# Attention maxima: one 512-key product of each key tile replaced by two 256-key products, one per row half, in one shared PSUM bank

## The chip, the cores and the metric

One NeuronCore of one Trainium2 chip. The metric is the device time of one execution in microseconds; lower is better. TensorE (PE in the profile) multiplies matrices into PSUM, which has eight banks of 128 partitions x 512 float32 here; VectorE (DVE) and ScalarE (ACT) read the banks; GpSimd (POOL) and SyncE (SP) do the rest, SP mostly by issuing DMAs.

## The reference

A transformer block on 2048 tokens of width 640: layer norm, attention with 32 heads of 20 columns, then layer norm and a gated feed-forward layer of width 1728. The part that matters here:

```
scores = jnp.einsum("bhqd,bhkd->bhqk", q, k) * (Dh ** -0.5)
p = _softmax(scores, axis=-1)
o = jnp.einsum("bhqk,bhkd->bhqd", p, v)
```

The softmax needs, for each head and each query, the maximum of its scores over all 2048 keys.

## The kernel before

**Units and steps.** The 32 heads lie in 8 groups (`g`) of four, and the 2048 queries in 4 chunks (`c`) of 512. A unit `u` is one group and one chunk, so there are 32 units (`NU`). A unit's attention runs over 16 tiles of 128 keys (`kt`, `NT = 16`); one unit and one key tile are one step, and `now[0] = u * 16 + kt` counts the 512 steps. The loop over `u` and `kt` stands at the end of the attention code.

**What a step does.** `scores` (L1387, L1393) multiplies 128 keys with 512 queries of one head into a bank, and ScalarE takes the exponential out of it into `probs`; four of these per step, one per head. `weigh` (L1397) multiplies the exponentials of the step before with the values, four heads side by side in four column groups of TensorE, into the accumulator bank. The maxima of *later* units are worked out in the same steps: `max_one` (L239, L245) multiplies 128 queries with 512 keys of one head into a bank and VectorE reduces the 512 columns to one maximum per query. There are 4 key chunks (`kc`) x 4 query tiles (`t`) x 2 pairs x 2 halves of such products in a unit; those that the projection stage has not already done stand in the list `rest`, 736 entries, each for both halves `b`, so 1472 products.

**Two row halves.** A head needs only 60 or 62 rows of TensorE's 128, so heads are stacked in two halves of 64 rows. A product on rows 0 to 63 (`b = 0`) and one on rows 64 to 127 (`b = 1`) can run at the same time. `weigh` takes all 128 rows, so it stands between the products of one step and the next.

**The order within a step** is a string. `s` and `S` are score products on half 0 and half 1, `m` and `M` maxima products on half 0 and half 1, `W` is `weigh` with the small work that goes with it. Three strings and their mirror images take turns (`ORDER`, L46), each with four scores and three maxima: one half has four products, the other three. Without maxima left the order is `sSsSW`. TensorE, ScalarE and VectorE each take their instructions in the order written.

**Banks.** Four banks go round among the scores (`one_places`), three among the maxima (`max_places`, `ps_max`), and one is the accumulator:

```
one_places, max_places, acc_place = places[:4], places[4:7], places[7]
```

`ps_max()` hands out the three maxima banks in turn. A product that is to write into a bank waits until VectorE's reduction of the bank's last content is over.

**From maxima to scores.** When the last maximum of unit `u` has been issued (`left[u] == 0`), `max_all` reduces the unit's table `mxs[u]` (128 x 16 x 4 numbers) on VectorE and splits the result on GpSimd; two or three steps later (`closing`) `max_finish` transposes it on TensorE (L264), copies it on ScalarE (L268) and writes it with four small DMAs on SP's queue (L273) into spare rows of the unit's query tile, which the unit's first scores need.

**Other work in the same steps.** SP's queue loads keys, values and queries of later units; GpSimd splits feed-forward weights (`preparing`); in the last units the output projection (`projection`, L1116) joins, and takes its banks from `ps_max` too.

## Time and profile before

| | |
|---|---|
| median of 3 runs | 2021.68 us (2021.38 to 2023.09) |
| span of the profiled execution | 2021.5 us |
| steps that hold maxima | from 321.8 us (first maxima product) to 1397.1 us (last reduction starts) |
| PE busy | 2003.8 us, 99% of the span |
| DVE, ACT busy | 1613.0 us (80%), 1458.9 us (72%) |
| maxima products / reductions | 1472 / 1472 |
| score products / exponentials | 2048 / 2048 |

The profile gives its execution no time apart from the span; the span is 0.2 us below the median of the runs. A line such as L245 is a line of the kernel printed above. PE is a matrix product, PEld the loading of its stationary operand. A busy PE is no proof that PE is the limit, because products overlap and their ends are modelled. In a row of the timeline the columns are: start, time from the first start to the last end, engine, line, operation, names, shapes, how many instructions were merged, and in brackets how long the engine was idle before and what ended that.

### The profile page before, as it was taken

Reading aid. Unit: us, or ns where it says so; the run is one execution under the profiler, and the core shown is the slowest. Engines: PE = TensorE matmul, PEld = TensorE weight load, DVE = VectorE, ACT = ScalarE, POOL = GpSimd, SP = SyncE. Lnnn points to the kernel's source line nnn. Section 1 sums busy time; section 2 is a strip of 40 time slices with the busy share of each in tenths; the row PEclk is TensorE's granted clock in tenths of the full one; section 3 lists DMA queues with packets and bytes.
Section 4 is the critical chain, followed back from the end, with each engine's and each line's share of the span. In section 5 each row is a group of like instructions: output and inputs, shape, how many; then the busy total and the mean of one; then the engine's idle time right before and its main releaser. Section 6 shows DMA issues by size and latency. Waiting matters only on the chain.

```text
span 2021.5 us, 39114 instructions
## 1 busy us (share of the span) xinstructions
PE 2003.8 (99%) x13714; PEld 1241.6 (61%) x13714; DVE 1613.0 (80%) x3250; ACT 1458.9 (72%) x2944; POOL 785.4 (39%) x1082
## 2 busy tenths in 40 slices
PE   8999999999999999999999999999999999999999
PEld 7999895333333333333333333345598888888888
DVE  8777787888888888888888888876388666676677
ACT  4888898999999999999999999987633222212221
POOL 4465451343424243344420011011156444764555
PEclk9999999999999999999999999999999999999999
DMA  7776562433433534435343122211158654974642
GB/s 235 256 229 200 179 196 78 137 120 119 148 125 107 160 113 140 142 121 173 115 139 98 36 70 74 80 62 49 51 190 313 208 189 154 353 273 157 205 150 93
DMA packets 205205, 304.91 MB, mean 151 GB/s; under 512 B 47648, under 2 KB 82720, under 8 KB 203984
## 3 DMA queue, kind: packets, MB, share of 16 engines
q1 hardware_dynamic: 204768, 302.24, 45.8%
q8 instruction: 109, 1.79, 0.4%
q14 instruction: 88, 0.72, 0.1%
q10 hardware_dynamic: 240, 0.17, 0.0%
HBM read 205.78 MB, written 95.68 MB: 149 GB/s over the span
## 4 chain that ended last, share of the span: by engine, by line
PE 94%; DVE 2%; DMA 1%; ACT 1%; POOL 1%; issue 1%; ACTq 0%; SPq 0%; POOLq 0%; DVEq 0%
PE banks L1397 25%; PE banks L1387 17%; PE banks L1565 16%; PE banks L239 12%; PE banks L574 9%; PE banks L1659 8%; PE banks L1116 3%; PE banks L218 3%; PE banks L195 1%; DMA xt<-in_A_x 0%; PE banks L838 0%; DMA z_d<-halves 0%; PE banks L264 0%; DVE st L133 0%; PE banks L795 0%
## 5 line engine op out<-in xcount | busy, mean ns | idle before, releaser
L1393 ACT ACTIVATE probs<-banks 128x512 f32<-128x512 f32 x2048 | 1056.2, 612 | 58.5 <-PE banks L1387 23.5
L245 DVE TENSOR_REDUCE mx<-banks 128x1 f32<-128x512 f32 x1472 | 925.5, 684 | 122.9 <-PE banks L239 75.9
L1387 PE MATMUL banks<-q_stk,k_stk 62*128 62x512 f32 x2048 | 581.5, 429 | 1.2 <-ACT probs L1393 1.1
L1397 PE MATMUL banks<-probs,v_stk 128*32 128x512 f32 x4096 | 544.3, 604 | 0.0
L239 PE MATMUL banks<-k_stk,q_stk 60*128 60x512 f32 x1472 | 486.8, 439 | 0.2
L1387 PEld LDWEIGHTS banks<-q_stk,k_stk 62*128 62x128 f32 x2048 | 290.6, 184 | 284.6 <-ACT probs L1393 270.8
L239 PEld LDWEIGHTS banks<-k_stk,q_stk 60*128 60x128 f32 x1472 | 244.2, 184 | 162.6 <-DVE mx L245 126.8
L1783 DVE TENSOR_TENSOR tmp<-banks,tmp 128x512 f32<-128x512 f32 x208 | 141.2, 689 | 114.4 <-PE banks L1565 88.9
L1397 PEld LDWEIGHTS banks<-probs,v_stk 128*32 128x32 f32 x4096 | 80.9, 108 | 182.1 <-issue 170.6
L1659 PE MATMUL banks<-halves,yp 128*128 128x320 f32 x1032 | 178.7, 308 | 0.2 <-DVE h L1664 0.2
L1659 PEld LDWEIGHTS banks<-halves,yp 128*128 128x128 f32 x1032 | 165.1, 188 | 16.0 <-DVE h L1664 0.5
L1565 PE MATMUL banks<-t,units 128*128 128x512 f32 x624 | 162.7, 396 | 0.1
L98 POOL TENSOR_TENSOR yp<-y,yp 128x256 fp32r<-128x256 f32 x96 | 60.3, 628 | 190.7 <-ACT yp L97 176.5
L1565 PE MATMUL banks<-z,units 128*128 128x512 f32 x516 | 133.9, 394 | 0.3 <-DVE tmp L1783 0.2
L256 POOL CAST both<-neg 128x16 fp32r<-128x16 f32 x32 | 6.6, 207 | 317.7 <-PE banks L239 141.4
L1565 PEld LDWEIGHTS banks<-t,units 128*128 128x128 f32 x624 | 112.5, 188 | 19.2 <-DVE tmp L1783 0.6
L1664 DVE TENSOR_TENSOR h<-banks,h 128x320 f32<-128x320 f32 x248 | 110.0, 481 | 8.6 <-POOL h L1697 4.4
L225 DVE CUSTOM_DVE_ANT_0 q_stk<-banks,q_stk 128x512 f32<-128x512 f32 x138 | 90.6, 687 | 32.4 <-PE banks L218 20.9
L574 PE MATMUL banks<-z_lo,w_hi 64*128 64x512 f32 x380 | 108.1, 394 | 0.0
L574 PE MATMUL banks<-z_hi,w_hi 64*128 64x512 f32 x380 | 105.3, 396 | 1.5 <-ACT z_hi L97 1.5
L1565 PEld LDWEIGHTS banks<-z,units 128*128 128x128 f32 x516 | 93.1, 187 | 16.7 <-DVE tmp L1783 0.5
L574 PE MATMUL banks<-z_hi,w_lo 64*128 64x512 f32 x380 | 101.8, 395 | 0.0
(212 smaller groups left out, 2903.6 us busy)
## 6 DMA issues: line engine op xcount, KB each, us to landing
units<-w_d SPq DMA_DIRECT2D x186, 256.0 KB
w_d<-stage SPq DMA_DIRECT2D x106, 256.0 KB
halves<-j_d SPq DMA_DIRECT2D x70, 320.0 KB
k_stk<-qk_d SPq DMA_DIRECT2D x112, 160.0 KB
j_d<-stage SPq DMA_DIRECT2D x42, 320.0 KB
q_stk<-qk_d SPq DMA_DIRECT2D x64, 160.0 KB
k_stk<-qk_d SPq DMA_DIRECT2D x112, 80.0 KB
rb<-r_d SPq DMA_DIRECT2D x32, 256.0 KB
```

The costliest lines, as they stand in the source:

```text
L218: nc.tensor.matmul(ps, q[rows, pair, t * P : (t + 1) * P], k[rows, pair, :], start=True, stop=True)
L225: nc.vector.tensor_tensor_reduce(out=place, in0=ps, in1=place, scale=1.0, scalar=LEAST, op0=ALU.add, op1=ALU.max, accum_out=mx[:, b, pair, ...
L239: nc.tensor.matmul(ps, queries[u][rows, pair, t * P : (t + 1) * P], keys[u // NC][rows, pair, kc * CH : (kc + 1) * CH], start=True, stop=True,
L245: nc.vector.tensor_reduce(mxs[u][:, b, pair, t, kc : kc + 1], ps, axis=AX.X, op=ALU.max)
L574: product = nc.tensor.matmul(job["ps"][:, :out], lhs, rhs, start=(half == 0 and i == 0), stop=(half == 1 and i == job["n"] - 1),)
L1387: nc.tensor.matmul(ps, keys[u // NC][rows, p, kt * P : (kt + 1) * P], queries[u][rows, p, :], start=True, stop=True,)
L1393: nc.scalar.activation(probs[p][:, b, :], ps, AF.Exp, scale=scale)
L1397: nc.tensor.matmul(acc[32 * j : 32 * j + 32, :], values[u // NC][:, kt, j * VW : j * VW + 32], probs[j // 2][:, j % 2, :], start=(kt == 0) ...
L1565: nc.tensor.matmul(ps.rearrange("p (t n) -> p t n", t=TPC), w[k][:, i], z[k][:, :, j], start=(first and m == 0), stop=(last and m == len(n ...
L1659: nc.tensor.matmul(ps, a, b, start=(n == 0), stop=(n == len(pairs) - 1))
L1664: nc.vector.tensor_tensor(out=h, in0=ps, in1=h, op=ALU.add)
L1783: add = lambda out, ps, x: nc.vector.tensor_tensor(out=out, in0=ps, in1=x, op=ALU.add)
```

## The change

The products of the last key chunk (`kc = 3`, 512 keys) are taken out of the list of whole products, except for the first three entries. Each of the other 245 entries (`in_parts`) covered its 512 keys with one product per half `b`. Now each is split into two entries of 256 keys (`part_pairs`, 490 in all), and an entry does both halves `b`: the product of half 1 goes into columns 256 to 511 of a bank (`max_half`), that of half 0 into columns 0 to 255 of the same bank, and one reduction (`max_halves`) turns the 2 x 256 columns into two maxima. The two products into one bank are kept apart in time by a no-operation on ScalarE's queue, which waits for the first product and for which the second waits (`behind`, moved up from the projection stage). The order of a step is now one string for all steps with maxima, `HsMsSmShW`: `H` starts an entry on half 1 (it takes the bank and issues the ScalarE no-operation), `h` ends it on half 0 and issues the reduction. So each step has, on either half, two scores, one whole maximum and one of 256 keys. `mxs[u]` has five columns for key chunks in place of four, and the tables of the units that the projection stage does not touch are allocated later, in another pool.

```diff
-ORDER = ("sMsSmSmW", "SmMsMsSW", "mSmMsSsW")
-ORDER += tuple(a.swapcase().replace("w", "W") for a in ORDER)
+ORDER = "HsMsSmShW"
+PART = NC - 1
+WHOLE = 3
...
+    def max_half(u, e, t, pair, b, ps):
+
+        rows = slice(b * ROW, b * ROW + NPART)
+        k0 = PART * CH + e * CH // 2
+        return nc.tensor.matmul(
+            ps[:, b * CH // 2 : (b + 1) * CH // 2],
+            queries[u][rows, pair, t * P : (t + 1) * P],
+            keys[u // NC][rows, pair, k0 : k0 + CH // 2],
+            start=True, stop=True,
+        )
+
+    def max_halves(u, e, t, pair, ps):
+
+        nc.vector.tensor_reduce(
+            mxs[u][:, :, pair, t, PART + e], ps.rearrange("p (b n) -> p b n", b=2),
+            axis=AX.X, op=ALU.max,
+        )
...
+    in_parts = [a for a in rest if a[1] == PART][WHOLE:]
+    wholes = [a for a in rest if a not in in_parts]
+    part_pairs = [(u, e, t, pair) for u, _, t, pair in in_parts for e in range(2)]
...
+    def next_half(b):
+        if not part_pairs:
+            return
+        if not halved:
+            ps = ps_max()
+            one = max_half(*part_pairs[0], b, ps).ins
+            between = nc.scalar.nop().ins
+            behind(between, one)
+            halved.append((ps, between))
+            return
+        a, (ps, between) = part_pairs.pop(0), halved.pop()
+        behind(max_half(*a, b, ps).ins, between)
+        max_halves(*a, ps)
+        counted(a[0])
...
-            order = ORDER[now[0] % len(ORDER)] if now[0] and (singles[0] or singles[1]) else "sSsSW"
+            order = ORDER if now[0] and (singles[0] or part_pairs) else "sSsSW"
             for op in order:
                 if op in "mM":
                     next_max(int(op == "M"))
+                elif op in "hH":
+                    next_half(int(op == "H"))
```

## The prediction

> **What bounds the kernel now.** I read the page's groups first, then windows, then the timeline of a few steps. Five groups make up a step.

> ```profile
> L1393 ACT ACTIVATE probs<-banks 128x512 f32<-128x512 f32 x2048 | 1056.2, 612 | 58.5 <-PE banks L1387 23.5
> L245 DVE TENSOR_REDUCE mx<-banks 128x1 f32<-128x512 f32 x1472 | 925.5, 684 | 122.9 <-PE banks L239 75.9
> L1387 PE MATMUL banks<-q_stk,k_stk 62*128 62x512 f32 x2048 | 581.5, 429 | 1.2 <-ACT probs L1393 1.1
> L1397 PE MATMUL banks<-probs,v_stk 128*32 128x512 f32 x4096 | 544.3, 604 | 0.0
> L239 PE MATMUL banks<-k_stk,q_stk 60*128 60x512 f32 x1472 | 486.8, 439 | 0.2
> ```

> The windows (busy time of PE, PEld, DVE, ACT and POOL in turn, or of one line alone) show TensorE without a gap, ScalarE at 97% and VectorE at 88%. All three are close to the limit, so an edit here can move the bound.

> ```profile
> 400.00:1300.00 900.00, 899.89 (x6321) 353.87 (x6323) 799.33 (x1312) 877.05 (x1731) 288.66 (x492) 1.00 0.36 114
> 323.50:1355.00 1031.50, 904.56 (x1439) 1.00 0.36 112
> 1355.00:1398.00 43.00, 19.83 (x32) 1.00 0.23 72
> ```

> The last two rows are L245 alone. 1439 reductions at three a step are 479.7 steps in 1031.5 us: 2.150 us a step. The other 32 fall into the late units, where the output projection makes steps longer. Now one step:

> ```profile
> 972.44 0.73 PE L239 MATMUL banks<-k_stk,q_stk 60*128 60x512 f32 x2
> 972.79 0.39 PE L1387 MATMUL banks<-q_stk,k_stk 62*128 62x512 f32 x1
> 973.00 1.89 DVE L245 TENSOR_REDUCE mx<-banks 128x1 f32<-128x512 f32 x3 [0.24 <-PE banks L239]
> 973.55 1.06 PE L1397 MATMUL banks<-probs,v_stk 128*32 128x512 f32 x8
> 974.54 0.18 PEld L239 LDWEIGHTS banks<-k_stk,q_stk 60*128 60x128 f32 x1 [0.84 <-DVE mx L245]
> 974.55 0.50 PE L239 MATMUL banks<-k_stk,q_stk 60*128 60x512 f32 x1
> 974.65 0.47 PEld L239 LDWEIGHTS banks<-k_stk,q_stk 60*128 60x128 f32 x2
> 974.89 0.55 PE L239 MATMUL banks<-k_stk,q_stk 60*128 60x512 f32 x2
> 975.00 0.22 DVE L252 TENSOR_REDUCE neg<-mx 128x16 f32<-128x64 f32 x1
> 975.14 1.88 DVE L245 TENSOR_REDUCE mx<-banks 128x1 f32<-128x512 f32 x3
> 975.12 0.62 PE L1387 MATMUL banks<-q_stk,k_stk 62*128 62x512 f32 x3
> ```

> The step runs from its first product (972.44) to the next step's (974.55), 2.11 us: 1.11 of products, then `weigh` at 973.55 for 1.00. Two things are to be seen. First, the row half with four products sets the 1.11. Second, VectorE's three reductions end at 973.00 + 1.89 = 974.89, 0.34 us *after* the next step has begun. Of the three products of that step only the third needs the bank of that last reduction: its weight load is the second of the pair that spans 974.65 to 975.12, so it began 0.18 before 975.12, at 974.94, 0.05 after the reduction's end. With three banks and three maxima a step, each position in the order always gets the same bank back, and the third position is late enough for it.

> **The change part by part.**

> *Product work.* On one half the deepest column of products goes from four of 512 to three of 512 and one of 256. The rows of 512 columns and of 320 (two of the timeline, one of the page) price that.

> ```profile
> 803.63 0.63 PE L239 MATMUL banks<-k_stk,q_stk 60*128 60x512 f32 x2
> 1352.30 1.00 PE L1116 MATMUL banks<-wo_hi,o_hi 128*128 128x320 f32 x5
> 1353.14 0.46 PE L1116 MATMUL banks<-wo_lo,o_hi 128*128 128x320 f32 x2
> L1116 PE MATMUL banks<-wo_lo,o_hi 128*128 128x320 f32 x160 | 28.6, 309 | 0.0
> ```

> The two products of 803.63 are on one half; with 0.39 us for the last (one product by itself, 972.79) they start 0.63 - 0.39 = 0.24 apart. For 320 columns it is 0.46 - 0.31 = 0.15. So a column costs 0.09/192 us and 256 columns start the next product 0.12 us later: 0.12 us a step is to be had on TensorE, if TensorE alone sets the step.

> *The bank and its place in the order.* `H` is the first instruction of a step, and it writes into the bank whose reduction is the *last* of the step before (`max_halves` is issued at `h`, behind the reductions of `M` and `m`). Banks go H, M, m, H, M, m, so H of step n+1 waits for the third reduction of step n. TensorE takes its instructions in order, so the scores and `M` stand behind H. Two places in the trace show that a wait holds back the other half too:

> ```profile
> 1350.39 0.18 PEld L1387 LDWEIGHTS banks<-q_stk,k_stk 62*128 62x128 f32 x1 [0.19 <-ACT probs L1393]
> 1350.39 0.18 PEld L239 LDWEIGHTS banks<-k_stk,q_stk 60*128 60x128 f32 x1
> 1395.48 0.18 PEld L239 LDWEIGHTS banks<-k_stk,q_stk 60*128 60x128 f32 x1 [0.21 <-DVE mx L245]
> 1395.48 0.29 PEld L1387 LDWEIGHTS banks<-q_stk,k_stk 62*128 62x128 f32 x3
> ```

> At 1350.39 a maxima product starts only when the score product ahead of it has its bank; at 1395.48 three scores start only with the maxima product that waited for VectorE. So the change closes a ring: third reduction, H, M behind it, first reduction, second, third. The step can't be shorter than that ring:

> 1. H's start to M's start, same half. With 320 columns the first two starts lie 0.24 apart (five in 1.00, less 0.31 for the last and 3 x 0.15), with 512 columns 0.73 - 0.39 = 0.34. On that line 256 columns give 0.21; as the rows are rounded I take 0.22. The ends are 0.21 and 0.34.
> 2. M to its end: 0.39.
> 3. End to first reduction: 972.44 + 0.50 to 973.00, 0.06. Ends 0.04 and 0.08, the rounding of the rows.
> 4. Three reductions: 1.89. The third now writes 2 x 1 from 2 x 256; the L252 row gives 16 outputs from 64 elements in 0.22, so outputs are nearly free. I take 0 more, ends 0 and 0.05.
> 5. Reduction's end to the weight load of H: 0.05.

> Sum 0.22 + 0.39 + 0.06 + 1.89 + 0.05 = 2.61 us, ends 2.58 and 2.80, against 2.150 now.

> *What lies beside the ring.* Products end about 1.1 us and `weigh` about 2.0 us after H, 0.6 before the next H, so the 0.12 us saved is lost in idle time. ScalarE's four exponentials need 2.06 us for four in its tightest row, below, less than 2.61. The L252 reduction (0.22) and other short VectorE work of a unit fall between the third reduction and the next first one, 0.05 + 0.22 + 0.39 + 0.06 = 0.72 us in which VectorE is idle.

> ```profile
> 1439.92 2.06 ACT L1393 ACTIVATE probs<-banks 128x512 f32<-128x512 f32 x4 [1.00 <-PE banks L1387]
> L1393 ACTq EVENT_SEMAPHORE  x4: 17/38/38, 320.7 to 320.9; - x4
> ```

> *The no-operation.* The trace has none; ScalarE's semaphore instructions took 17 to 38 ns. It stands ahead of the step's exponentials and waits for H, which ends before the first score does, so exponentials lose nothing but those 0.04 us, in idle time. `h` waits for it; H is over about 0.4 us after its start, and `h` is fourth on its half, at 0.34 + 2 x 0.24 = 0.82. Behind `h` stands `weigh`, which would delay the next H only if it began after 2.6 - 1.0 = 1.6 us, and the third reduction (due at 0.67 + 1.2 = 1.9). So the cost is 0 unless the no-operation answers some 0.7 us late; the other end is what that would add, at most one exponential, 0.5 us a step.

> *Moved and added.* The maxima of a unit now end 5 or 6 steps before its scores start, and `max_finish` comes 3 or 4 steps before; until now that was 3 to 18 (counted through the code's own rule). Its four DMAs (about 0.63 us of SP each) now stand at key tile 12 or 13 of every unit, behind or beside the key and value loads at tiles 8 to 14.

> ```profile
> L273 SPq DMA_DIRECT2D q_stk<-m x128: 621/635/947, 268.1 to 1405.8; - x128
> ```

> Four take 2.5 us of 8 us or more; six of the 31 units have three steps already, at 2.15 us each, and steps are about to be longer. I take 0; a unit's late query would cost a microsecond, 31 us at most. The tables' 80 columns in place of 64 lengthen the L252 reduction alone, which is hidden; where they are allocated costs nothing that a row shows.

> *Sum.* 479.7 steps x (2.61 - 2.150 = 0.46) = 221. The last 10.7 steps hold projection work which takes maxima banks also; there between 0 and 0.46 is added, 5 at most; I take 4. Everything before 322 us and after the maxima stays. 221 + 4 = +225; span 2021.5 + 225 = 2246.5, and with the 0.2 us to the median of the runs 2246.7, so 2247 us. Ends: 0.43 x 479.7 = +206, so 2228; 0.60 x 479.7 + 5 = +293, so 2315 (0.60 leaves out the topmost 0.05 of the ring, since not all its terms lie at the high end at once).

> [...]

> **The rivals.**

> 1. *Faster: H's bank is free in time.* Then the better balance is all that counts: 0.12 x 490 = 59 us less, 1963 us; ScalarE's 2.06 and VectorE's 1.89 would just allow 2.03 a step. It decides if the third reduction ends by H's start, that is within about 2.0 us of the step's start; the row of 973.00 has it at 974.89, 2.45 after its step's start, and the new one can't be earlier, since `h` is issued last. Against it also the 0.05 us between release and load. Chance 0.06.
> 2. *Slower, but by less: the weight load of H goes ahead of the wait.* The second load follows the first by 0.11 us (974.54, 974.65), so that much leaves the ring: 2.50 a step, 0.35 x 479.7 + 3 = +171, 2193 us. Chance 0.04.
> 3. *Slower by more: the clock falls.* TensorE would idle 0.6 of 2.6 us in every step.

> ```profile
> 211.00:214.00 3.00, 1.86 (x19) 1.28 (x18) 0.00 (x0) 2.94 (x8) 2.47 (x3) 1.00 0.70 184
> 214.00:221.00 7.00, 6.66 (x37) 6.19 (x39) 1.44 (x5) 3.28 (x7) 5.10 (x5) 0.51 0.55 187
> 2014.40:2017.80 3.40, 2.40 (x17) 2.14 (x15) 2.93 (x7) 0.00 (x0) 0.00 (x0) 1.00 1.02 390
> ```

> After 1.86 busy of 3.00 us the granted clock was 0.51 for 7 us; with 2.40 of 3.40 busy (0.71) it stayed 1.00. The new step would be 2.0 of 2.6 busy, 0.77, on the safe side, but not by much. If it fell, a step would take 2 x 2.0 = 4 us in such spells; half the steps so would be (4.0 + 2.61)/2 = 3.3, +1.15 x 490 = +564, 2586 us. Chance 0.04. [...]
> 4. *No change*: the idle time is absorbed and the balance gives nothing. Nothing in the rows speaks for it; 2021.7, chance 0.02.
> 5. *Slower by more: `h` is late at the no-operation*, by up to 0.5 us a step: 3.1 a step, +0.95 x 490 = +466, 2487 us. Against it the slack of 0.7 us. Chance 0.04.

> **How the numbers follow.** The forecast, the ring, has the remaining chance, 0.80, nearly all of it between 2228 and 2315, which is the range. What a measurement of this kernel can tell from no change is about 0.2% (4 us). Faster: 0.06 (rival 1). Same: 0.02 (rival 4). Slower: 0.92 (the ring and rivals 2, 3 and 5).

> **What would show it.** Steps of 2.6 us in the timeline; three reductions back to back, then some 0.7 us in which VectorE is idle and waits for a product of L239; TensorE idle about 0.6 us a step, the weight load of `max_half` waiting for the reduction of `max_halves`, scores starting together with it; ScalarE's busy share down from 97% to about 80%; projection stage and feed-forward as before. Wrong it is if the load of `H` doesn't wait for VectorE, or if steps are shorter than three reductions and one product, 2.3 us.

## The result and the profile after

The changed kernel takes 2259.2 us (median of 4 runs, 2255.8 to 2260.3) against 2022.3 before (by now four runs): ratio 1.117, 95% interval 1.115 to 1.118. The span of its profiled execution is 2257.8 us. From here on lines are those of the changed kernel: L265 is `max_half`, L274 `max_halves`, L251 and L257 product and reduction of a whole maximum, L1417 and L1423 score and exponential, L1427 `weigh`, L1437 ScalarE's copy of the accumulator, L1499 the no-operation. `ACTq` and `SPq` are the queues of ScalarE and SyncE.

The page's groups, with the idle time before each and what ended it in the last columns:

```profile
L1423 ACT ACTIVATE probs<-banks 128x512 f32<-128x512 f32 x2048 | 1057.6, 604 | 288.5 <-PE banks L1417 270.6
L257 DVE TENSOR_REDUCE mx<-banks 128x1 f32<-128x512 f32 x982 | 632.5, 686 | 348.4 <-PE banks L251 339.8
L265 PEld LDWEIGHTS banks<-k_stk,q_stk 60*128 60x128 f32 x980 | 182.2, 186 | 656.5 <-DVE mx L274 648.4
L265 PE MATMUL banks<-k_stk,q_stk 60*128 60x256 f32 x980 | 323.6, 330 | 237.1 <-DVE mx L274 234.6
L274 DVE TENSOR_REDUCE mx<-banks 128x2 f32<-128x512 f32 x490 | 334.1, 682 | 0.5 <-PE banks L265 0.5
```

ScalarE was idle for 58.5 us before its exponentials, now for 288.5; VectorE idles 348 us for the whole maxima's products, TensorE 235 us for L274, the reduction of the shared bank. Engines that were all near their limit now wait for each other in turn. The chain that ended last, followed back through what each piece of work waited for, says the same. Its shares by engine, after and before:

```profile
PE 40%; DVE 37%; issue 2%; DMA 2%; SPq 1%; ACT 1%; POOL 0%; DVEq 0%; ACTq 0%; POOLq 0%
PE 94%; DVE 2%; DMA 1%; ACT 1%; POOL 1%; issue 1%; ACTq 0%; SPq 0%; POOLq 0%; DVEq 0%
```

Windows (L274 alone, then all engines; the third number from the end is the granted clock of TensorE) and, in a second block, one step of the timeline:

```profile
500.00:780.00 280.00, 73.64 (x108) 1.00 0.36 108
400.00:1500.00 1100.00, 886.15 (x6731) 393.00 (x6730) 800.79 (x1309) 881.06 (x1729) 287.35 (x490) 0.99 0.31 95
```

```profile
1001.77 0.18 PEld L265 LDWEIGHTS banks<-k_stk,q_stk 60*128 60x128 f32 x1 [1.41 <-DVE mx L274]
1001.78 0.38 PE L265 MATMUL banks<-k_stk,q_stk 60*128 60x256 f32 x1 [0.50 <-DVE mx L274]
1001.78 0.18 PEld L1417 LDWEIGHTS banks<-q_stk,k_stk 62*128 62x128 f32 x1
1002.00 0.39 PE L251 MATMUL banks<-k_stk,q_stk 60*128 60x512 f32 x1
1002.42 1.29 DVE L257 TENSOR_REDUCE mx<-banks 128x1 f32<-128x512 f32 x2 [0.70 <-PE banks L251]
1002.59 0.28 PE L265 MATMUL banks<-k_stk,q_stk 60*128 60x256 f32 x1
1002.79 1.06 PE L1427 MATMUL banks<-probs,v_stk 128*32 128x512 f32 x8
1003.63 0.68 DVE L274 TENSOR_REDUCE mx<-banks 128x2 f32<-128x512 f32 x1
1004.36 0.18 PEld L265 LDWEIGHTS banks<-k_stk,q_stk 60*128 60x128 f32 x1 [1.42 <-DVE mx L274]
```

280 us with 108 shared banks are 2.593 us a step, against 2.150 before. The ring can be read off the rows: H at 1001.78, M behind it at 1002.00, its end 1002.39, first reduction 1002.42, the shared bank's reduction 1003.63 to 1004.31, next H's load 1004.36. The score of the other half starts with H and runs beside it (1001.78 to 1002.28, H to 1002.16).

### The profile page after: what moved, and what is told of

It is laid out like the page before. It is cut to its first block, busy times and chain, and to the rows that moved or that the text cites. A ratio compares the mean times of both kernels' runs of the same rounds, so it can differ in the third digit from the quotient of the medians.

```text
span 2257.8 us, 40600 instructions
## 1 busy us (share of the span) xinstructions
PE 1986.7 (88%) x14204; PEld 1287.0 (57%) x14204; DVE 1610.7 (71%) x3250; ACT 1463.3 (65%) x2944; POOL 785.5 (35%) x1082
## 4 chain that ended last, share of the span: by engine, by line
PE 40%; DVE 37%; issue 2%; DMA 2%; SPq 1%; ACT 1%; POOL 0%; DVEq 0%; ACTq 0%; POOLq 0%
DVE mx L257 25%; PE banks L1619 15%; DVE mx L274 12%; PE banks L1713 8%; PE banks L265 7%; PE banks L1417 3%; PE banks L1146 3%; PE banks L251 3%; PE banks L1427 1%; DMA q_stk<-qk_d 1%; SPq L1440 0%; ACT probs L1423 0%; DMA o_t<-o_d 0%; DMA raw<-in_B_w_up 0%; SPq L303 0%
## 5 line engine op out<-in xcount | busy, mean ns | idle before, releaser
L1423 ACT ACTIVATE probs<-banks 128x512 f32<-128x512 f32 x2048 | 1057.6, 604 | 288.5 <-PE banks L1417 270.6
L257 DVE TENSOR_REDUCE mx<-banks 128x1 f32<-128x512 f32 x982 | 632.5, 686 | 348.4 <-PE banks L251 339.8
L265 PEld LDWEIGHTS banks<-k_stk,q_stk 60*128 60x128 f32 x980 | 182.2, 186 | 656.5 <-DVE mx L274 648.4
L1417 PE MATMUL banks<-q_stk,k_stk 62*128 62x512 f32 x2048 | 552.1, 422 | 0.9 <-ACT probs L1423 0.9
L1427 PE MATMUL banks<-probs,v_stk 128*32 128x512 f32 x4096 | 548.3, 608 | 0.0
L265 PE MATMUL banks<-k_stk,q_stk 60*128 60x256 f32 x980 | 323.6, 330 | 237.1 <-DVE mx L274 234.6
L251 PE MATMUL banks<-k_stk,q_stk 60*128 60x512 f32 x982 | 370.9, 396 | 8.4 <-DMA q_stk<-qk_d 8.3
L274 DVE TENSOR_REDUCE mx<-banks 128x2 f32<-128x512 f32 x490 | 334.1, 682 | 0.5 <-PE banks L265 0.5
L1417 PEld LDWEIGHTS banks<-q_stk,k_stk 62*128 62x128 f32 x2048 | 301.8, 186 | 11.9 <-ACT probs L1423 9.1
L251 PEld LDWEIGHTS banks<-k_stk,q_stk 60*128 60x128 f32 x982 | 183.0, 187 | 11.7 <-DMA q_stk<-qk_d 9.2
L1462 POOL TENSOR_TENSOR o<-o,rb 128x512 f32<-128x512 f32 x31 | 39.8, 1283 | 378.1 <-DMA rb<-r_d 164.8
L1427 PEld LDWEIGHTS banks<-probs,v_stk 128*32 128x32 f32 x4096 | 81.1, 108 | 132.4 <-issue 131.2
```

The costliest lines, as they stand in the source:

```text
L251: nc.tensor.matmul(ps, queries[u][rows, pair, t * P : (t + 1) * P], keys[u // NC][rows, pair, kc * CH : (kc + 1) * CH], start=True, stop=True,
L257: nc.vector.tensor_reduce(mxs[u][:, b, pair, t, kc : kc + 1], ps, axis=AX.X, op=ALU.max)
L265: return nc.tensor.matmul(ps[:, b * CH // 2 : (b + 1) * CH // 2], queries[u][rows, pair, t * P : (t + 1) * P], keys[u // NC][rows, pair, k ...
L274: nc.vector.tensor_reduce(mxs[u][:, :, pair, t, PART + e], ps.rearrange("p (b n) -> p b n", b=2), axis=AX.X, op=ALU.max,)
L1417: nc.tensor.matmul(ps, keys[u // NC][rows, p, kt * P : (kt + 1) * P], queries[u][rows, p, :], start=True, stop=True,)
L1423: nc.scalar.activation(probs[p][:, b, :], ps, AF.Exp, scale=scale)
```

## The experiments

**Is it the ring or the shared bank?** The first pair of runs takes one of the two away and keeps the other.

Shared bank and no-operation kept, but the shared bank's reduction between the two others:

```diff
-ORDER = "HsMsSmShW"
+ORDER = "HsMshSSmW"
```

> The changed kernel with the order string HsMshSSmW in place of HsMsSmShW: same products, same no-operation, but h and with it the reduction of the shared bank stands between the reductions of M and m. Ring theory (the first product of a step waits for the last reduction of the step before): the shared bank's reduction then ends about 1.95 us after the step's start, so H no longer waits; the step falls from 2.59 to 2.0 to 2.1 us, TensorE's own length, and the time to about 1980 us (1965 to 2010), below the kernel before. Rival theory (the shared bank itself costs: the second product waits for the no-operation, and ScalarE is held up): the same waits are all there, the step stays at 2.4 us or more, the time above 2180 us.

Measured: 2057.8 us, ratio to the kernel before 1.017 (1.016 to 1.019). Some 200 us are gone with nothing but the order changed, so the ring theory holds and its rival falls. But the time is above the 1965 to 2010 us expected: the step did not come down to 2.0 to 2.1 us, and units 3, 11 and 19, of which more below, took some 20 us longer than the others. A window (L274 alone) and the rows of a step show why the step is long:

```profile
500.00:700.00 200.00, 63.47 (x93) 1.00 0.45 138
```

```profile
902.53 0.18 PEld L265 LDWEIGHTS banks<-k_stk,q_stk 60*128 60x128 f32 x1 [0.84 <-DVE mx L274]
903.02 0.18 PEld L265 LDWEIGHTS banks<-k_stk,q_stk 60*128 60x128 f32 x1 [0.19 <-ACTq L1499]
903.02 0.18 PEld L1417 LDWEIGHTS banks<-q_stk,k_stk 62*128 62x128 f32 x1
903.67 0.16 PEld L1427 LDWEIGHTS banks<-probs,v_stk 128*32 128x32 f32 x8 [0.36 <-issue]
```

200/93 = 2.15 us. `h`'s load at 903.02 waited 0.19 us for the no-operation, the score behind it waited with it, and `weigh` began 1.14 us after H's load (903.67 - 902.53); in the changed kernel it is 1.02 (1002.79 - 1001.77). So the no-operation has a price after all when `h` stands early. (The bracket at 902.53 names the release that came last by the profile. It did not hold H: that reduction had ended at 902.33. What H stands behind here is `weigh`: it comes 1.00 us after `weigh`'s start, 903.67 to 904.67 in the next step. The same bracket, with 0.84, in the rows of later runs is to be read so, too.)

The ring kept, but no shared bank, no halves, no no-operation: the kernel before, with the first product of a step (whole, halves in turn) reduced last.

```diff
-ORDER = ("sMsSmSmW", "SmMsMsSW", "mSmMsSsW")
+ORDER = ("HsMsSmShW",)
...
+    def next_begun(b):
+        if begun:
+            a, ps = begun.pop()
+            max_reduce(*a, ps)
+            counted(a)
+        elif singles[b]:
+            a = singles[b].pop(0)
+            begun.append((a, max_product(*a)))
```

> The kernel before, with whole products of 512 keys only, no shared bank and no no-operation, but in the order of the change: the first product of a step is a whole maxima product (half 1 and half 0 in turn) whose reduction is issued last, at h. Ring theory: the ring is there without any half, and longer by the 0.12 us of the longer first product: 2.71 us a step, 0.56 x 490 = +275, about 2297 us (2270 to 2315). Rival theory (shared bank and no-operation are the cost): steps as before, 2.15 us, about 2022 us (2010 to 2050).

Measured: 2295.3 us in one run. In its timeline (its own line numbers: L243 the maxima product, L253 the reduction) H's load follows H's load by 2.71 us, as worked out:

```profile
1000.91 0.18 PEld L243 LDWEIGHTS banks<-k_stk,q_stk 60*128 60x128 f32 x1 [1.43 <-DVE mx L253]
1001.68 1.89 DVE L253 TENSOR_REDUCE mx<-banks 128x1 f32<-128x512 f32 x3 [0.82 <-PE banks L1395]
1003.62 0.18 PEld L243 LDWEIGHTS banks<-k_stk,q_stk 60*128 60x128 f32 x1 [1.43 <-DVE mx L253]
```

The slow-down thus comes whole without any part of the shared bank.

**Does VectorE's time lie in the ring?**

```diff
+        nc.vector.tensor_reduce(idle_out, ident[:, :MORE], axis=AX.X, op=ALU.max)
         nc.vector.tensor_reduce(
             mxs[u][:, :, pair, t, PART + e], ps.rearrange("p (b n) -> p b n", b=2),
```

> The changed kernel with one more VectorE reduction (128 columns of the identity, result not used) ahead of each reduction of a shared bank, 490 in all. From 512 columns at 0.60 us start to start it should take about 0.20. Ring theory: it lies in the ring and each step grows by all of it, 0.20 x 490 = +98, about 2357 us (2340 to 2370). Rival theory (VectorE idles 0.7 us a step, so it is not the bound): it goes into the idle time, 2259 us within 10.

Measured: 2351.7 us in one run, +92.5, or 0.19 us for each of the 490. From its timeline (L277 the extra reduction, L278 that of the shared bank):

```profile
1002.42 0.28 DVE L277 TENSOR_REDUCE idle_out<-ident 128x1 f32<-128x128 f32 x1
1002.62 0.68 DVE L278 TENSOR_REDUCE mx<-banks 128x2 f32<-128x512 f32 x1
```

From start to start it takes 0.20. VectorE idles 0.7 us in each step, and yet what it gets more to do lengthens the step by all of it: its idle time is a wait *inside* the ring, not spare.

**Units 3, 11 and 19.** By the starts of their first scores, units take 41.5 us, but these three 47.5, 46.1 and 44.1. The kernel before has no such units. The timeline shows a whole maximum waiting for the queries of the unit three ahead:

```profile
446.93 2.48 SPq L1440 DMA_DIRECT2D r<-o  x4
449.50 0.53 SPq L1226 DMA_DIRECT2D w_d<-stage  x1
450.07 0.44 SPq L1255 DMA_DIRECT2D raw<-in_B_w_gate  x1
450.56 0.61 SPq L1255 DMA_DIRECT2D raw<-in_B_w_up  x1
451.27 1.55 SPq L170 DMA_DIRECT2D q_stk<-qk_d  x4
458.43 0.28 PEld L251 LDWEIGHTS banks<-k_stk,q_stk 60*128 60x128 f32 x1 [4.12 <-DMA q_stk<-qk_d]
```

```diff
-            if kt == 2 and u + 3 < NU:
+            if kt == 0 and u + 3 < NU:
```

> The changed kernel with the load of unit u+3's queries issued at key tile 0 in place of 2. Theory: units 3, 11 and 19 took 5.8, 4.4 and 2.4 us longer than the others since the whole maxima products now reach the unit three ahead while its queries are still landing; with 5 us more the wait is gone: -12.6 us, 2246.5 us, ratio to the kernel before 1.1105. Rival: the wait is SP's queue, or the slot is not free earlier, and nothing changes: 2259 us.

Measured: 2258.9 us, ratio 1.117 (1.115 to 1.118): nothing to be seen in the time. The rival was right as to the queue. The load stood two key tiles earlier in the program, but in units 3 and 11 behind the same four transfers `r<-o`, the same store and the same two weight loads, so it was issued no earlier, as this row of unit 3 shows. Only in unit 19 did it pass a store; that unit took 42.0 us in place of 44.1.

```profile
451.22 1.56 SPq L170 DMA_DIRECT2D q_stk<-qk_d  x4
```

What stood ahead in the queue were the four transfers, 446.93 to 449.41: they start when ScalarE's copy of the accumulator (446.27 to 446.90) is over, and the store follows them at 449.50. It did not wait for GpSimd, as the next expectation has it; GpSimd had nothing to do from 438.6 to 455.9. The next run puts the load ahead of all of these, which the freed slot allows as soon as unit `u`'s last scores are issued.

```diff
-            if kt == 2 and u + 3 < NU:
+            if kt == 2 and u == 0:
                 load_queries(u + 3)
+            if kt == NT - 1 and u + 4 < NU:
+                load_queries(u + 4)
```

> The changed kernel (order HsMsSmShW), but with the load of unit u+4's queries issued at the end of key tile 15 of unit u, ahead of the weight stores and loads that stand in SP's queue at key tile 0. At key tile 0 the load of units 3, 11 and 19 still stood behind a store that waited for GpSimd and behind two weight loads, and landed at the same time as before. Theory (late queries are those 12.6 us): units 3, 11 and 19 take 41.5 us like the others, the half-clock spells at 458, 796 and 1130 us are gone, 2246 us (2242 to 2250). Rival (the wait is for something else that lands then): 2259 us.

Measured: 2246.3 us, ratio 1.109 (1.107 to 1.111), 12.9 us less. In its timeline the load stands at 445.13, ahead of the transfers and the store, no whole maximum waits for queries, and units 3, 11 and 19 take 41.5 us like the others.

```profile
445.13 1.59 SPq L170 DMA_DIRECT2D q_stk<-qk_d  x4
451.05 0.54 SPq L1226 DMA_DIRECT2D w_d<-stage  x1
```

**What the change could be worth without the ring.** First the order that leaves `h` time for the no-operation, then that with the earlier query load.

```diff
-ORDER = "HsMsSmShW"
+ORDER = "HsMsShSmW"
```

> The changed kernel with the order string HsMsShSmW. In the order HsMshSSmW the step was 2.15 us: h's weight load waited 0.18 us for the no-operation, the score S behind it waited with it, and the weighing began 1.14 us after the step's start in place of 1.02. Here S stands ahead of h. Theory (that wait held back the queue, and TensorE now sets the step): h still starts at 0.5 to 0.6 us but nothing else is late, the step falls to 2.02 to 2.05 us; with the waits for queries in units 3, 11 and 19, which last some 18 us at this step length, about 1990 us (1975 to 2005), faster than before. Rival (ScalarE or VectorE already sets 2.14): the step stays, 2058 us within 8.

Measured: 2020.2 us, ratio 0.997 (0.996 to 0.998). So the order of the first experiment was held back by where `h` stood, but the step is 190/91 = 2.09 us, not 2.02 to 2.05 (a window of L274), and the time is outside what was expected.

```profile
500.00:690.00 190.00, 62.10 (x91) 1.00 0.45 140
```

> Order HsMsShSmW and the query load at key tile 15 together. Theory: steps of 2.02 to 2.05 us without the three waits, 490 x 0.11 = 54 us below the kernel before, about 1970 us (1960 to 1985). Rival (VectorE's 1.89 us and ScalarE's four exponentials do not fit a step of 2.03 in practice): 2010 us or more.

Measured: 2005.2 us, ratio 0.989 (0.988 to 0.991): 1.1% faster than the kernel before, but by less than half of the 54 us that were worked out. Steps of 2.03 us are there (901.24 to 903.27), but between longer ones. In the window below the rows ScalarE, the fourth of the five engines, is busy for 890.7 of 900 us:

```profile
901.24 0.18 PEld L265 LDWEIGHTS banks<-k_stk,q_stk 60*128 60x128 f32 x1 [0.84 <-DVE mx L274]
903.27 0.18 PEld L265 LDWEIGHTS banks<-k_stk,q_stk 60*128 60x128 f32 x1 [0.84 <-DVE mx L274]
903.90 0.18 PEld L1417 LDWEIGHTS banks<-q_stk,k_stk 62*128 62x128 f32 x1
905.39 0.18 PEld L265 LDWEIGHTS banks<-k_stk,q_stk 60*128 60x128 f32 x1 [0.84 <-DVE mx L274]
```

```profile
400.00:1300.00 900.00, 895.99 (x6904) 382.53 (x6899) 818.86 (x1344) 890.74 (x1773) 290.24 (x493) 1.00 0.38 118
```

> The kernel of the last run (query load at key tile 15) with the order string HsMsShmSW in place of HsMsShSmW: the fourth score stands behind m. In the last run steps of 2.02 and of 2.12 us took turns, mean 2.09; in a long one the load of the fourth score began 0.05 us after the end of the fourth exponential of the step before (903.85), whose bank it takes, and m behind it came late too. Theory (that wait is what is left of the difference to TensorE's 2.02): in last place the fourth score needs its bank only some 0.1 us later, when it is free, and m no longer stands behind it; steps of 2.02 to 2.04 us, 0.05 x 490 = 24 us less, about 1982 us (1975 to 1992). Rival (VectorE with 0.2 us to spare a step, or ScalarE itself, sets 2.09): 2005 us within 5.

Measured: 2003.5 us, ratio 0.990 (0.988 to 0.992), no difference to the run before that can be told. The alternation is gone (steps of 2.03 to 2.06), yet the mean is 280/135 = 2.07 in this window of L274; the timeline rows below it hold a long step:

```profile
500.00:780.00 280.00, 92.14 (x135) 1.00 0.43 135
```

```profile
890.40 0.63 ACT L1437 ACTIVATE o<-banks 128x512 f32<-128x512 f32 x1
890.87 6.20 ACT L1423 ACTIVATE probs<-banks 128x512 f32<-128x512 f32 x12
892.08 0.18 PEld L265 LDWEIGHTS banks<-k_stk,q_stk 60*128 60x128 f32 x1 [0.84 <-DVE mx L274]
892.55 0.18 PEld L1417 LDWEIGHTS banks<-q_stk,k_stk 62*128 62x128 f32 x1 [0.18 <-ACT probs L1423]
893.04 0.18 PEld L1417 LDWEIGHTS banks<-q_stk,k_stk 62*128 62x128 f32 x1 [0.18 <-ACT probs L1423]
894.46 0.18 PEld L265 LDWEIGHTS banks<-k_stk,q_stk 60*128 60x128 f32 x1 [0.84 <-DVE mx L274]
```

Once in a unit ScalarE copies the accumulator (L1437), falls behind by one instruction, and the scores of the next step wait for its banks: 2.38 us from 892.08 to 894.46. The rival was nearer: with the ring gone ScalarE, whose twelve exponentials from 890.87 on follow each other without a gap for 6.20 us, is by these rows the next bound. No run took the copy away.

## Why the prediction was right

The forecast was 2247 us within 2228 to 2315, the measurement 2259; the mechanism is shown by the runs with whole products and with the longer ring, the price by the rows.

- *The ring.* Its terms came out as 0.22 (H to M), 0.39 (M), 0.03 (to the first reduction), 1.89 (1002.42 to 1004.31) and 0.05, which within the rounding of the rows is the 2.59 measured; 2.61 was forecast. Only the third term was sized too large, by 0.02 to 0.03 (M ends at 1002.39, the reduction starts at 1002.42); why it is shorter here no run settles. Over 479.7 steps that is 213 us where 221 stood.
- *Product work.* Of the 0.12 us a step the rows show 0.09: `weigh` now starts 1.02 us after H's load, where it came 1.11 us after the step's first product. They are hidden, as forecast, and came to light only without the ring.
- *The no-operation* costs nothing in the regular steps of the change, as said: of the 490 only one, at 1577.22 below, shows TensorE waiting for it, for 1.0 us. The reason, that `h` stands fourth, is what the first experiment showed from the other side: there `h` stood earlier, `weigh` came 0.12 us later, and the step was 2.15 us, where it was 2.09 with the score ahead of `h`.
- *Moved and added* is the step that failed. It looked at the maxima's end (`max_finish`) and took 0; the other end was overlooked. With the last key chunk taken out of the list of whole products, that list reaches a new unit earlier, three times before its queries have landed: counted through the code's own rule, in units 3, 11 and 19 the first whole maximum of the unit three ahead now comes 2 steps behind the load of its queries, where it came 9 behind. These units are 6.0, 4.6 and 2.6 us longer than the others, 13 in all, and the run with the load ahead of the stores is 12.9 us faster.
- *The last steps* were put at 4 us. Eight of them with projection work took 5.4 to 5.8 us in place of 4.5 to 4.8, about 6 in all: the projection's bank, too, comes from the three and waits for L274, for which TensorE stood idle 5.9 us at these eight places. One more, just ahead, lost 1.5 us in a way listed as a rival: ScalarE stood at an activation that waited for a load, and the no-operation behind it kept `h` and `weigh` waiting.

```profile
1577.14 0.74 ACT L105 ACTIVATE o_hi<-o_t 128x640 fp32r<-128x640 f32 x1 [1.98 <-DMA o_t<-o_d]
1577.22 0.18 PEld L265 LDWEIGHTS banks<-k_stk,q_stk 60*128 60x128 f32 x1 [1.42 <-ACTq L1499]
1587.77 1.00 PE L1146 MATMUL banks<-wo_hi,o_hi 128*128 128x320 f32 x5 [0.70 <-DVE mx L274]
```

So 213 + 13 + 6 + 2 = 234 of the 236.3 us between the two spans. That the 225 of the forecast came so near is in part luck: a ring sized a little too long, by 8 us in all, made up for part of what was missed.

- *The rivals.* The load of H did not go ahead of its wait: it starts 0.05 us after the reduction's end in the step shown (1004.31 to 1004.36). The clock did not fall in the regular steps: from 500 to 780 us, with TensorE busy for 226 of 280 us, it was 1.00.

## What to carry to other kernels

When a step uses as many buffers as it has, each position in its order gets the same buffer back; add up what lies between the release of the last buffer and the first instruction of the next step that needs it, through every engine, before moving an instruction to the front. That one instruction was here the gate for everything behind it in its queue (the other half's score started with H, at 1001.78), and the cheapest mend was to reorder, to release early what is needed first: the order alone took 2259 us to 2058 and to 2020 us. And when work leaves a queue, look at what moves forward in it, not only at what it delays.

## What was not expected of the hardware

```profile
454.00:458.00 4.00, 0.51 (x2) 0.19 (x2) 0.07 (x1) 0.73 (x2) 1.98 (x3) 1.00 0.56 152
458.00:465.00 7.00, 6.54 (x30) 2.64 (x30) 3.98 (x7) 3.64 (x7) 4.34 (x10) 0.51 0.03 6
```

The four us of waiting were followed by seven at a granted clock of 0.51. In the run with the earlier query load the window of that stretch shows 1.00:

```profile
453.00:493.00 40.00, 32.49 (x249) 14.80 (x249) 29.08 (x49) 32.10 (x64) 13.45 (x25) 1.00 0.27 87
```

Three shorter spells at half clock, from 796, 1130 and 1578 us on (0.51, 0.51 and 0.50 in windows of 2.0, 2.5 and 2.0 us), followed the other two waits for queries, in which TensorE was idle for 3.23 and 1.24 us, and the wait for the no-operation at 1577.22, before which it had been idle for 0.98 us only. Which rule the clock goes by no run here settles.
